# A quarter of an FFT stage moved into the first FFN group, and casts and PSUM emptyings handed to other engines

## The chip, the cores and the metric

One core of a Trainium2 chip. The metric is the device time of one execution in microseconds (us). Each run lists the mean granted TensorE clock, and executions with a mean of 1.000 are some 1.3 us shorter than those with 0.998. "Full-clock runs" below are those with 1.000; where a tenth of a per cent matters I compare these alone.

## The reference, cut to what matters

```python
X = np.fft.rfft(x, axis=1)                       # x: 8 batches x 3008 x 256
Y = X * (filt_r + 1j * filt_i)[None]
y = np.fft.irfft(Y, n=3008, axis=1).astype(np.float32)
h = np.maximum(y.reshape(24064, 256) @ w_in, 0)  # w_in: 256 x 2048
return (h * h @ w_out).astype(np.float32)        # w_out: 2048 x 256
```

## The kernel before

The FFT is done by matmuls in stages: A (x to u, through memory), B (u to the spectrum, times the filter: "products"), P (products to ze, through memory as dZ), Y (zt to yt). The FFN is done in groups of 512 tokens with 8 slots each: first layer (psH), relu on ScalarE, squaring on VectorE, second layer (psO, TensorE). TensorE leaves its results in PSUM tiles, which ScalarE or VectorE then "empties", that is, copies into a tile in SBUF. The code calls a piece of 512 fp32 columns of such a tile a "bank". The FFN of one batch hides the FFT of the next. Only the start is exposed: batch 0's FFT, three quarters of stage A of batch 1, and FFN group 0, whose first layer has no second layer beside it. The parts that the change and the argument touch:

```python
p_u = ctx.enter_context(tc.tile_pool(name="p_u", bufs=3))   # u tiles, and the two sSPx tables
def psF(name): ...   # [128, 512] fp32, 2 buffers;  psO: likewise 2;  psH: [128, 2, 512], 2 buffers

def place_f(im, k, *engs, rotate=False):       # builds 4 columns of the filter, Fr or Fi
    ...
        t = psH(f"psf_{im}_{k}")
        banks, groups = [t[:, 0, :], t[:, 1, :]], [(t, 0)]
    ...                                        # matmuls into the two banks
    for t, i in groups:                        # each group emptied by engs[i % len(engs)]
        ...

def unit_a(b, a):                              # one sixteenth of stage A
    c, i = divmod(a, 4)
    if i == 0:
        us[(b, c)] = p_u.tile([96, 8, D], F16, tag="u", name=f"u_{b}_{c}")
    ps = psF(f"psA_{b}_{a}")
    ...                                        # two matmuls
    if a % 2 == 0: nc.scalar.copy(out=o, in_=pv)
    else:          nc.vector.tensor_copy(out=o, in_=pv)
    if i == 3: write_u(b, c)

# in the plan of batch 1, by slot (0 to 7 are group 0):
            for k in range(4):
                put((4, 5, 7, 7)[k], 1, cast_wout, k, nc.vector)
        t0 = 2 if b == 1 else 6
        for a in range(12 if b == 1 else 0, 16):
            put(t0 + a // 2, a % 2, unit_a, b, a)          # units 12 to 15: slots 8 and 9

# the start:
    for k in range(7):
        ...                                                # unit_b, place_f(1, ..), unit_p0
        if k < 4:
            place_f(0, k + 2, nc.scalar)                   # an Fr bank
    cast_wide(1, 2, nc.vector, nc.scalar)
    read_z(0, 0); load_wout(0); read_z(0, 1); load_wout(1) # zt, and 2 MB of W_out
    for c in (0, 2, 1): chunk_a(1, c)                      # stage A of batch 1, chunks 0, 2, 1
    for c in (0, 2, 1): write_u(1, c)
    for n in range(4): unit_y(0, n)
```

Of the kernel before, what the change touches and what calls it, by code (L numbers as in the profile page):

```python
# [110 lines left out]
def kernel(  # L111
# [9 lines left out]
    nc = tc.nc  # L121
    B, S, D = x.shape
# [34 lines left out]
    def psF(name):  # L157
        return pps.tile([128, 512], F32, tag="psF", name=name, bufs=2)

    def psO(name):  # L160
        return pps.tile([128, 2, 256], F32, tag="psO", name=name, bufs=2)

    def psH(name):
        return pps.tile([128, 2, 512], F32, tag="psH", name=name, bufs=2)
# [4 lines left out]
    def bank_pair(name):  # L169

        k = npair[0] % 4
        npair[0] += 1
        if k < 2:
            t = psH(name)
            return [t[:, 0, :], t[:, 1, :]], [(t, 0)]
        ts = [psF(f"{name}_{i}") if k == 2 else psO(f"{name}_{i}").rearrange("p a d -> p (a d)")
              for i in range(2)]
        return ts, [(t.unsqueeze(1), i) for i, t in enumerate(ts)]
# [42 lines left out]
    def cast(eng, out, in_):  # L221
        (eng.copy if eng is nc.scalar else eng.tensor_copy)(out=out, in_=in_)

    def cast_wide(b, k, *engs):
        t = p_x16.tile([128, 8, D], F16, tag="x16", name=f"xw16_{b}_{k}")
        for i in range(2):
            m = slice(4 * i, 4 * i + 4)
            cast(engs[i], t[:, m, :], xw32[(b, k)][:, m, :])
        xw16[(b, k)] = t
# [36 lines left out]
    ps = psO("warm").rearrange("p a d -> p (a d)")  # L266
# [2 lines left out]

    f16s = []  # L270

    def place_f(im, k, *engs, rotate=False):

        if rotate:
            banks, groups = bank_pair(f"psf_{im}_{k}")
        else:
            t = psH(f"psf_{im}_{k}")
            banks, groups = [t[:, 0, :], t[:, 1, :]], [(t, 0)]
        for i in range(4):
            c = 4 * k + i  # L280
            e0, e1 = D * c, D * (47 - c)
            cuts = [0] + [d for d in range(1, D)
                          if (e0 + d) % QF == 0 or (c and (e1 + d) % QF == 0)] + [D]
            for d0, d1 in zip(cuts, cuts[1:]):
                o = banks[i // 2][:, (i % 2) * D + d0:(i % 2) * D + d1]
                q, a = divmod(e0 + d0, QF)
                nc.tensor.matmul(o, sPF[:, PQ.index((0, q)), :], f16s[0][:, im, a:a + d1 - d0],  # L287
                                 start=True, stop=False)
                q, a = divmod(e1 + d0, QF) if c else (0, QF + d0)
                nc.tensor.matmul(o, sPF[:, PQ.index((1, q)), :], f16s[0][:, im, a:a + d1 - d0],  # L290
                                 start=False, stop=True)
        for t, i in groups:
            n = t.shape[1]
            eng = engs[i % len(engs)]
            dst = sF[:, im, 4 * k + 2 * i:4 * k + 2 * i + 2 * n, :]
            src = t.rearrange("p t (a d) -> p (t a) d", d=D)
            if eng is nc.scalar:
                eng.activation(out=dst, in_=src, func=AF.Copy, scale=sign[:, 0:1] if im else 1.0)  # L298
            elif im:
                eng.tensor_scalar_mul(out=dst, in0=src, scalar1=sign[:, 0:1])  # L300
            else:
                eng.tensor_copy(out=dst, in_=src)
# [15 lines left out]
    def cast_win():  # L318
        for t, k, c in wins:
            nc.gpsimd.tensor_copy(out=sWin[:, k, c], in_=t)  # L320
# [22 lines left out]
    def write_u(b, c):  # L343
        nc.sync.dma_start(
            out=dU[b].rearrange("(m q) d -> q m d", q=96)[:, 8 * c:8 * c + 8, :],
            in_=us.pop((b, c)))

    def unit_a(b, a):
# [5 lines that stand above are left out]
        m = slice(2 * i, 2 * i + 2)  # L354
        if b == 1:
            nc.tensor.matmul(ps[0:96, :], s1[:, c // 2, :], xw16[(b, 2 * (c % 2))][:, m, :],
                             start=True, stop=False)
            nc.tensor.matmul(ps[0:96, :], s1[0:120, 2 + c, :], xw16[(b, 1)][0:120, m, :],
                             start=False, stop=True)
        else:  # L360
            nc.tensor.matmul(ps[0:96, :], sSA, x16s[(b, c)][:, m, :], start=True, stop=True)  # L361
        o = us[(b, c)][:, 2 * i:2 * i + 2, :]
        pv = ps[0:96, :].rearrange("p (a d) -> p a d", d=D)
        if a % 2 == 0:
            nc.scalar.copy(out=o, in_=pv)  # L365
        else:
            nc.vector.tensor_copy(out=o, in_=pv)  # L367
        if i == 3:
            write_u(b, c)
# [102 lines left out]
    def unit_p0(k):  # L472

        if k == 0:
            zes[0] = p_h2.tile([128, NC, D], F16, tag="h2", name="ze_0")
        ze = zes[0][:, 4 * k:4 * k + 4, :]
        ps = psH(f"psP_0_{k}")
        for i in range(4):
            c2 = 4 * k + i
            prod = prods[(0, c2 // 2)]  # L480
            for v, w in enumerate((sSP[:, c2, :], sSPx[c2 // 12][:, c2 % 12, :])):
                nc.tensor.matmul(ps[:, i // 2, (i % 2) * D:(i % 2) * D + D], w,
                                 prod[:, v, i % 2, :], start=(v == 0), stop=(v == 1))
        nc.scalar.copy(out=ze, in_=ps.rearrange("p t (a d) -> p (t a) d", d=D))
        nc.sync.dma_start(
            out=dZ[0].rearrange("(s p) d -> p s d", p=128)[:, 4 * k:4 * k + 4, :],
            in_=ze)
# [22 lines left out]
    def read_z(b, c, ks=(0, 1)):  # L510
        zt = ztiles[c]
        v = dZ[b].rearrange("(q j) d -> q j d", j=NM)
        for k in ks:
            nc.sync.dma_start(out=zt[64 * k:64 * k + 48],
                              in_=v[48 * k:48 * k + 48, 8 * c:8 * c + 8, :])
        zts[(b, c)] = zt
# [93 lines left out]
    def fft_plan(b):  # L610

        plan = {}

        def put(r, place, f, *a):
            plan.setdefault((r, place), []).append((f, a))

        if b == 1:
            for n in range(4, 16):
                put(n if n < 8 else n + 2 if n < 12 else 2 * n - 7, n % 2, unit_y, 0, n)
            for k in range(4):  # L620
                put((4, 5, 7, 7)[k], 1, cast_wout, k, nc.vector)
        t0 = 2 if b == 1 else 6
        for a in range(12 if b == 1 else 0, 16):
            put(t0 + a // 2, a % 2, unit_a, b, a)
        put(10 if b == 1 else 14, 1, read_u, b)
        t0 = 14 if b == 1 else 19
        for p in range(12):
            r = t0 + (17 if b == 1 else 18) * p // 11
            put(r, 0, unit_b, b, p)
            put(r, 0, unit_s, b, p)  # L630
            put(r + 2, 1, unit_p, b, p)
        t0 = 34 if b == 1 else 40
        for c in range(4):
            put(t0, 1, read_z, b, c)
        if b + 1 < B:
            for c in range(2):
                put(t0 - 13, 1, load_x, b + 1, c)
            for c in range(4):
                r = t0 - 8 + 3 * c
                put(r, 1, cast_x, b + 1, c)  # L640
                if c < 2:
                    put(r, 1, load_x, b + 1, c + 2)
        for n in range(16):
            put((38 if b == 1 else 45) + n // 2, n % 2, unit_y, b, n)
        return plan
# [32 lines left out]
    turn_u(2, nc.scalar)  # L678
    turn_u(3, nc.vector)
    place_f(0, 0, nc.scalar, rotate=True)  # L680
    for eng, e in ((nc.vector, slice(0, 1024)), (nc.gpsimd, slice(1024, 2048)),
                   (nc.scalar, slice(2048, QF))):
        cast(eng, f16s[0][:, 1, e], f32s[1][:, e])
    turn_u(4, nc.vector)
    place_f(0, 1, nc.scalar, rotate=True)
    turn_u(5, nc.vector)
    place_f(1, 0, nc.scalar, nc.vector, rotate=True)
# [4 lines left out]
        nc.gpsimd.tensor_copy(out=sSPx[-1][0:64, o, :], in_=sSP[64:128, c, :])  # L692
        nc.gpsimd.tensor_copy(out=sSPx[-1][64:128, o, :], in_=sSP[0:64, c, :])
    cast_win()
    for k in range(2):
        cast_wide(1, k, nc.gpsimd, nc.gpsimd)
    for k in range(7):
        if k < 6:
            unit_b(0, 2 * k)
            if k < 5:  # L700
                place_f(1, k + 1, nc.scalar)
            unit_b(0, 2 * k + 1)
        if k > 0:
            unit_p0(k - 1)
        if k < 4:
            place_f(0, k + 2, nc.scalar)
    cast_wide(1, 2, nc.vector, nc.scalar)
    read_z(0, 0)
    load_wout(0)
    read_z(0, 1)  # L710
# [17 lines left out]
    for s in range((NG + 1) * SLOTS):  # L728
        g, k = divmod(s, SLOTS)
# [40 lines left out]
```

## Time and profile before

The median at the prediction was 794.04 us (793.07 to 794.68, 3 runs).

| event in the trace of before | us |
|---|---|
| twelfth product of batch 0 ends | 40.40 |
| last store of ze (dZ) landed | 44.49 |
| first psY matmul; first psH matmul | 48.26; 49.71 |
| last W_out landed; chunk 0 of u written | 56.35; 57.59 |
| second psH matmul of group 1 (the row "x3") | 59.76 |
| first product of batch 1 | 73.74 |
| span | 791.9 |

A landing is the sixteenth increment of a transfer's semaphore.

One more view, ScalarE's timeline in batch 0's loop (columns: start, duration, engine, line, operation, output and input, shape, count; a bracket holds the idle time before it and what ended it):

```profile
28.83 1.02 ACT L298 ACTIVATE sF<-psf 128x1024 f16<-128x1024 f32 x1
29.93 1.11 ACT L298 ACTIVATE sF<-psf,sign 128x1024 f16<-128x1024 f32 x1
31.02 1.01 ACT L484 CAST ze<-psP 128x1024 f16<-128x1024 f32 x1
```

A whole Fr bank pair, a Fi bank pair and a ze, without a gap: 3.14 us of each cycle of 3.33. That is what the change wants to shorten.

### The profile page before, as it was taken

To read this page: it belongs to the slowest core of one execution; us is meant where nothing else is said; L and a number is where in the kernel's file an instruction comes from. 1 tells how busy PE (TensorE), PEld (TensorE's weight loads), DVE (VectorE), ACT (ScalarE), POOL (GpSimd) and SP (SyncE) were. 2 spreads that over 40 slices of the span, in tenths; PEclk is the share of its full clock that TensorE was granted. 3 is DMA by queue.
4 is the path that set the end of the run, shared out by engine and by line. 5 is a ranking of instruction groups with operands and counts; after the bars stand their busy time and mean duration, and the time that the engine had idled before them with its cause. 6 is when DMAs were issued, how large, how long until landed. Compare 5 with 4: busy or idle time off the path is not lost.

```text
span 791.9 us, 14822 instructions
## 1 busy us (share of the span) xinstructions
PE 778.9 (98%) x6102; PEld 552.5 (70%) x6102; DVE 550.3 (69%) x897; ACT 557.4 (70%) x711; POOL 23.6 (3%) x36
## 2 busy tenths in 40 slices
PE   8989999999999999999999999999999999999998
PEld 5746667667676777867777676776767677676666
DVE  6866994579755897559965699556995579553342
ACT  3976776777777777767776777676777777776664
POOL 3800000000000000000000000000000000000000
PEclk9999999999999999999999999999999999999999
DMA  9994554346814557154562555424563332611111
GB/s 363 368 260 153 146 157 111 93 135 167 205 42 112 167 155 180 48 173 135 132 167 65 163 147 155 112 80 148 159 180 86 97 133 66 147 40 41 41 41 54
DMA packets 88571, 107.32 MB, mean 136 GB/s; under 512 B 6336, under 2 KB 79040, under 8 KB 84288
## 3 DMA queue, kind: packets, MB, share of 16 engines
q1 hardware_dynamic: 88296, 106.19, 46.5%
q8 instruction: 48, 0.79, 0.4%
q10 hardware_dynamic: 144, 0.18, 0.1%
q14 instruction: 19, 0.16, 0.1%
q0 software_dynamic: 64, 0.00, 0.0%
HBM read 58.12 MB, written 48.23 MB: 134 GB/s over the span
## 4 chain that ended last, share of the span: by engine, by line
PE 89%; DVE 6%; DMA 3%; ACT 1%; SPq 0%; issue 0%; DVEq 0%; ACTq 0%
PE psO L579 40%; PE psH L562 38%; PE psA L361 3%; PE psY L532 2%; PE psB L445 2%; DMA f<-in_filt_i_dram 2%; PE psP L496 2%; DVE prod L453 2%; DVE h L570 1%; DMA wout<-in_moe_w_out_dram 1%; PE psf L287 1%; PE psf L290 1%; DVE yf L467 0%; ACT sF L298 0%; DVE yf L461 0%; ACT h L566 0%
## 5 line engine op out<-in xcount | busy, mean ns | idle before, releaser
L566 ACT ACTIVATE h<-psH 128x1024 f16<-128x1024 f32 x376 | 384.9, 1024 | 189.3 <-PE psH L562 186.7
L579 PE MATMUL psO<-sWout,h 128*128 128x256 f16 x3008 | 388.9, 272 | 0.6 <-DVE h L570 0.6
L562 PE MATMUL psH<-yt,sWin 128*128 128x512 f16 (+7 forms) x1728 | 386.9, 351 | 1.6 <-DVE yt L541 0.7
L579 PEld LDWEIGHTS <-h 128*128 128x128 f16 x3008 | 290.6, 98 | 79.1 <-DVE h L570 0.9
L570 DVE TENSOR_TENSOR h<-h 128x1024 f16<-128x1024 f16 x376 | 252.6, 685 | 104.7 <-ACT h L566 104.5
L562 PEld LDWEIGHTS <-sWin 128*128 128x128 f16 x1728 | 159.5, 98 | 101.7 <-issue 3.3
L453 DVE TENSOR_TENSOR prod<-psB,sF 128x1024 f16<-128x1024 f32 x84 | 102.3, 1218 | 2.8 <-PE psB L445 2.8
L541 DVE CAST yt<-psY 128x376 f16<-128x376 f32 x62 | 34.0, 549 | 59.4 <-PE psY L532 59.4
L367 DVE CAST u<-psA 96x512 f16<-96x512 f32 x50 | 34.3, 687 | 47.3 <-PE psA L361 45.1
L498 ACT CAST ze<-psP 128x512 f16<-128x512 f32 x84 | 49.1, 585 | 17.2 <-PE psP L496 14.7
L590 ACT COPY ost<-psO 128x512 f32<-128x512 f32 (+1 forms) x96 | 55.8, 581 | 6.8 <-PE psO L579 5.3
L532 PE MATMUL psY<-sC,zt 112*128 112x94 f16 x512 | 42.4, 205 | 1.4 <-DMA zt<-dZ 1.4
L532 PEld LDWEIGHTS <-zt 112*128 112x128 f16 x512 | 35.1, 98 | 11.6 <-issue 1.6
L467 DVE TENSOR_TENSOR yf<-prod,yf 128x512 f16<-128x512 f16 x84 | 35.7, 425 | 2.9
L361 PE MATMUL psA<-x,sC 94*96 94x512 f16 x96 | 36.6, 382 | 0.0
L445 PE MATMUL psB<-ut,sSB 128*128 128x256 f16 x192 | 36.5, 273 | 0.0
L496 PE MATMUL psP<-yf,sSP 128*128 128x256 f16 x168 | 32.1, 272 | 0.5 <-DVE prod L453 0.3
L539 ACT CAST yt<-psY 128x376 f16<-128x376 f32 x66 | 30.9, 468 | 2.0 <-issue 1.7
L445 PEld LDWEIGHTS <-sSB 128*128 128x128 f16 x192 | 18.5, 98 | 19.5
L340 DVE CAST x<-x 94x2048 f16<-94x2048 f32 x24 | 29.2, 1216 | 0.0
L365 ACT CAST u<-psA 96x512 f16<-96x512 f32 x50 | 28.6, 572 | 0.0
L460 DVE COPY yf<-prod 64x512 f16<-64x512 f16 x84 | 24.3, 289 | 2.9
(65 smaller groups left out, 253.2 us busy)
## 6 DMA issues: line engine op xcount, KB each, us to landing
x<-in_x_dram SPq DMA_DIRECT2D x20, 768.0 KB
zt<-dZ SPq DMA_DIRECT2D x64, 192.0 KB
dU<-u SPq DMA_DIRECT2D x28, 384.0 KB
dZ<-ze SPq DMA_DIRECT2D x28, 384.0 KB
out_dram<-ost SPq DMA_DIRECT2D x66, 128.0 KB
out_dram<-ost SPq DMA_DIRECT2D x31, 256.0 KB
ut<-dU SPq DMA_DIRECT2D x7, 1024.0 KB
xw<-in_x_dram SPq DMA_DIRECT2D x6, 1024.0 KB
```

Of the source, the lines that this page charges most:

```text
L361: nc.tensor.matmul(ps[0:96, :], sSA, x16s[(b, c)][:, m, :], start=True, stop=True)
L445: nc.tensor.matmul(ps[:, i * D:(i + 1) * D], sSB[:, 2 * p + i, :], uts[b][:, 2 * p + i, :], start=True, stop=True)
L453: nc.vector.tensor_mul(out=prod, in0=ps.rearrange("p (a d) -> p a d", d=D).unsqueeze(1).to_broadcast([128, 2, 2, D]), in1=sF[:, :, 2 * p:2 ...
L467: nc.vector.tensor_add(out=yf, in0=prod[:, 0], in1=yf)
L496: nc.tensor.matmul(ps[:, i * D:(i + 1) * D], sSP[:, 2 * p + i, :], yf[:, i, :], start=True, stop=True)
L498: nc.scalar.copy(out=zes[(b, c)][:, 2 * i6:2 * i6 + 2, :], in_=ps.rearrange("p (a d) -> p a d", d=D))
L532: nc.tensor.matmul(ps[:, 94 * jj:94 * jj + 94], zt[:, 4 * (g % 2) + jj, dt * 128:(dt + 1) * 128], sSY, start=True, stop=True)
L562: nc.tensor.matmul(ps[:, i, o:o + n], sWin[:, dt, jt * 128:(jt + 1) * 128], yts[b][:, dt, r:r + n], start=(dt == 0), stop=(dt == 1))
L566: nc.scalar.activation(out=h2[:, 2 * s:2 * s + 2, :], in_=ps, func=AF.Relu)
L570: nc.vector.tensor_mul(out=v, in0=v, in1=v)
L579: nc.tensor.matmul(pso[g][:, t % 2, :], h2s[g][:, jt, t * 128:(t + 1) * 128], sWout[:, jt, :], start=(jt == 0), stop=(jt == NJT - 1))
L590: nc.scalar.copy(out=ost[:, h0:h0 + step, :], in_=pso[g][:, h0:h0 + step, :])
```

## The change

Its intent: (1) share the Fr banks, and the last ze, between ScalarE and VectorE, and put the last x casts on idle GpSimd, so that batch 0's spectrum ends sooner; (2) take the W_out casts from VectorE to GpSimd; (3) run units 12 to 15 of stage A in slots 1 to 4 of group 0, where TensorE has holes, instead of in slots 8 and 9, where it is full. All four of these units are then emptied by VectorE (before, ScalarE took two of them), and four psY units come two slots earlier.

```diff
-    def place_f(im, k, *engs, rotate=False):
+    def place_f(im, k, *engs, rotate=False, halves=False):
...
-            banks, groups = [t[:, 0, :], t[:, 1, :]], [(t, 0)]
+            banks = [t[:, 0, :], t[:, 1, :]]
+            groups = [(t[:, i:i + 1, :], i) for i in range(2)] if halves else [(t, 0)]
...                                              (unit_a)
-        if a % 2 == 0:
+        if a % 2 == 0 and b > 1:
             nc.scalar.copy(out=o, in_=pv)
...                                              (unit_p0: the last ze)
-        ps = psH(f"psP_0_{k}")
+        if k == 5:
+            ps = [psF("psP_0_5a"), psF("psP_0_5b")]
...                                              (for k < 5 as before: one psH tile, emptied by ScalarE)
-        nc.scalar.copy(out=ze, in_=ps.rearrange("p t (a d) -> p (t a) d", d=D))
+        else:
+            nc.scalar.copy(out=ze[:, 0:2, :], in_=ps[0].rearrange("p (a d) -> p a d", d=D))
+            nc.scalar.copy(out=ze[:, 2, :], in_=ps[1][:, 0:D])
+            nc.vector.tensor_copy(out=ze[:, 3, :], in_=ps[1][:, D:2 * D])
...                                              (the plan of batch 1)
-                put(n if n < 8 else n + 2 if n < 12 else 2 * n - 7, n % 2, unit_y, 0, n)
+                put(n if n < 12 else 2 * n - 7, n % 2, unit_y, 0, n)
-                put((4, 5, 7, 7)[k], 1, cast_wout, k, nc.vector)
-        t0 = 2 if b == 1 else 6
+                put((1, 2, 4, 5)[k], 1, cast_wout, k, nc.gpsimd)
+        t0 = 6
-            put(t0 + a // 2, a % 2, unit_a, b, a)
+            put(a - 11 if b == 1 else t0 + a // 2, a % 2, unit_a, b, a)
...                                              (the start)
-    for k in range(2):
+    for k in range(3):
         cast_wide(1, k, nc.gpsimd, nc.gpsimd)
-            place_f(0, k + 2, nc.scalar)
-    cast_wide(1, 2, nc.vector, nc.scalar)
+            place_f(0, k + 2, nc.scalar, nc.vector, halves=True)
```

More of the change, by code (lines that the diff above doesn't have):

```diff
@@ L476, in unit_p0 @@
         ze = zes[0][:, 4 * k:4 * k + 4, :]
-        ps = psH(f"psP_0_{k}")
+        if k == 5:
+            ps = [psF("psP_0_5a"), psF("psP_0_5b")]
+        else:
+            t = psH(f"psP_0_{k}")
+            ps = [t[:, 0, :], t[:, 1, :]]
         for i in range(4):
@@ L481, in unit_p0 @@
             for v, w in enumerate((sSP[:, c2, :], sSPx[c2 // 12][:, c2 % 12, :])):
-                nc.tensor.matmul(ps[:, i // 2, (i % 2) * D:(i % 2) * D + D], w,
+                nc.tensor.matmul(ps[i // 2][:, (i % 2) * D:(i % 2) * D + D], w,
                                  prod[:, v, i % 2, :], start=(v == 0), stop=(v == 1))
-        nc.scalar.copy(out=ze, in_=ps.rearrange("p t (a d) -> p (t a) d", d=D))
+        if k < 5:
+            nc.scalar.copy(out=ze, in_=t.rearrange("p t (a d) -> p (t a) d", d=D))
+        else:
+            nc.scalar.copy(out=ze[:, 0:2, :], in_=ps[0].rearrange("p (a d) -> p a d", d=D))
+            nc.scalar.copy(out=ze[:, 2, :], in_=ps[1][:, 0:D])
+            nc.vector.tensor_copy(out=ze[:, 3, :], in_=ps[1][:, D:2 * D])
         nc.sync.dma_start(
```

## The prediction

> **What bounds the kernel now.** I read the page first (busy shares and chain), then a table of engine busy time by stretch, then each engine's timeline from 22 to 75 us, because every line of the diff acts there. The page:
>
> ```profile
> PE 778.9 (98%) x6102; PEld 552.5 (70%) x6102; DVE 550.3 (69%) x897; ACT 557.4 (70%) x711; POOL 23.6 (3%) x36
> ...
> PE 89%; DVE 6%; DMA 3%; ACT 1%; SPq 0%; issue 0%; DVEq 0%; ACTq 0%
> ```
>
> TensorE sets the time: 89% of the chain that ended last. So a change in the first 75 us is worth what it does to the moment at which a given piece of the main TensorE stream is reached. The stretches:
>
> ```profile
> 22.00:32.00 10.00, 9.65 (x93) 8.27 (x94) 9.37 (x10) 9.02 (x10) 8.50 (x14) 1.00 1.04 412
> 32.00:42.00 10.00, 9.01 (x80) 7.24 (x78) 7.63 (x8) 8.22 (x10) 7.13 (x10) 1.00 0.78 278
> 42.00:49.70 7.70, 5.72 (x44) 3.48 (x43) 4.45 (x6) 5.01 (x9) 0.00 (x0) 1.00 0.74 202
> 49.70:59.80 10.10, 8.91 (x50) 4.07 (x50) 7.12 (x13) 8.40 (x10) 0.00 (x0) 1.00 1.11 315
> 59.80:73.20 13.40, 13.40 (x99) 8.90 (x99) 7.42 (x13) 8.28 (x11) 0.00 (x0) 1.00 0.46 138
> ```
>
> Columns: stretch, length, busy us of TensorE, its weight loads, VectorE, ScalarE, GpSimd, then clock, DMA share, GB/s. Three regimes. (a) 22 to 42, batch 0's spectrum (Fr/Fi banks, products, ze): TensorE, VectorE and ScalarE all 76 to 97% busy. (b) 42 to 49.7: TensorE waits for ze to go out to memory and come back as zt. (c) 49.7 to 59.8 is FFN group 0, with first matmuls alone, so TensorE has holes; from 59.8 it has none. The change moves TensorE work from the full stretch into the one with holes. The DMA share in (c), 1.11, is the highest: the queue is full just there.
>
> **What the Trainium skill says.** "VectorE: DVE Perf Modes", section "Why PSUM operands drop a tier": a PSUM operand in fp32 gets no speed-up. The trace agrees: a 96x512 VectorE emptying takes 0.69 us and a 128x1024 product 1.22, against 0.57 and 1.02 for ScalarE's emptying of these widths. "GPSIMD Engine Reference", section "4.1 Engine selection": one-input work is roughly line-rate there. The trace: four 128x1024 casts in 3.99 us, 1.0 each, against 0.68 on VectorE. "PSUM — Partial Sum Buffer", section "Engine vs sequencer instructions": the queues of ScalarE, VectorE and GpSimd are strict FIFO. I use that below; every timeline here agrees. "TensorE: Matmul & The Clock Gate", section "What's actually happening": after an idle window of about 3.4 us the clock can halve. Here the clock column is 1.00, and the longest TensorE wait in stretches (a) to (c) is 1.42 us, so this trace tests nothing of it; the changed kernel may.
>
> **Part 1, Fr banks and last ze on two engines, x casts to GpSimd (22 to 44 us).** VectorE before:
>
> ```profile
> 24.42 7.06 DVE L453 TENSOR_TENSOR prods<-psB,sF 128x1024 f16<-128x1024 f32 x6
> 32.44 2.35 DVE L453 TENSOR_TENSOR prods<-psB,sF 128x1024 f16<-128x1024 f32 x2 [0.96 <-ACT ze L484]
> 35.77 4.62 DVE L453 TENSOR_TENSOR prods<-psB,sF 128x1024 f16<-128x1024 f32 x4 [0.98 <-ACT ze L484]
> 40.30 0.68 DVE L222 CAST xw<-xw 128x1024 f16<-128x1024 f32 x1
> ```
>
> Twelve products (14.03 us) and 1.94 us of waits end at 40.40; then the last ze matmuls (0.6 us), one ScalarE emptying from 41.07 to 42.09, and the last store. Now VectorE also empties half of four Fr banks: 4 x 0.62 (0.69 alone, some 0.62 back to back, as in a pair of 1.28) = 2.5 us. The two waits hold only 1.9, so VectorE becomes the loop's bound: 24.42 + 14.03 + 2.5 = 40.95, about 0.1 more for small waits, 41.05: 0.65 later. ScalarE loses 4 x 0.45 (1.02 to 0.57), but the TensorE cycle of 3.33 us there runs through the emptying of the Fi bank (1.11), which stays whole. At the end the last ze is 256 columns on each engine, about 0.42 by extrapolation from 1.22 and 0.69, in place of 1.02: 0.60 earlier. Sum: +0.65 - 0.60, about nil. The x casts leave VectorE (0.68) and ScalarE (1.05), but lie in the wait for zt; on GpSimd they run from 39.14 to about 41.2, before their reader at about 45. Worth 0.
>
> **Part 2, W_out cast to GpSimd.** Four x 0.61 us leave VectorE in (c), where it was 70% busy. The last landing of W_out is at 56.35 (the sixteenth increment of its semaphore), so GpSimd ends near 58.4, before the first use. Worth nearly 0 by itself: the last yt emptying of group 0 waits for the squaring before it anyway.
>
> **Part 3, the quarter of stage A into group 0.** Gain: four units x 2 matmuls x 0.217 us = 1.74 us of TensorE leave the full stretch. Shifting four psY units within it changes no sum.
>
> The price is a buffer. The u tiles have 3 buffers and rotate: two hold the sSPx tables, then u of chunks 0, 2, 1, then chunk 3, the moved quarter. Chunk 3 therefore takes chunk 0's buffer and its first emptying must wait until chunk 0 has been written to memory. The compiled kernel before has just that wait on that instruction. It costs nothing there, since that emptying comes at 61.91. When does chunk 0 land?
>
> ```profile
> 45.05 0.39 SPq L328 DMA_DIRECT2D wout<-in_moe_w_out_dram  x1
> 45.49 1.03 SPq L514 DMA_DIRECT2D zt<-dZ  x2
> 46.57 0.43 SPq L328 DMA_DIRECT2D wout<-in_moe_w_out_dram  x1
> 47.10 7.71 SPq L344 DMA_DIRECT2D dU<-u  x3
> ```
>
> It is issued at 47.10, but behind 2 MB of W_out on one queue: its 512-byte packets start only at about 55.3, after the last of W_out, and the sixteenth increment of its semaphore comes at **57.59**. The change leaves that order alone. The moved unit 12 would be ready to be emptied at about 52, so VectorE stands from there to 57.59. Behind it, in order, stand squarings and yt emptyings. Unit 14 needs unit 12's PSUM bank (psF, two of them), so TensorE stops at it, from about 54.2. Compare TensorE before:
>
> ```profile
> 54.17 1.02 PE L562 MATMUL psH<-yt,sWin 128*128 128x512 f16 x4 [0.20 <-ACT h L566]
> ...
> 57.60 1.02 PE L562 MATMUL psH<-yt,sWin 128*128 128x512 f16 x4
> 58.46 0.33 PE L532 MATMUL psY<-sC,zt 112*128 112x94 f16 x4
> 58.88 0.38 PE L562 MATMUL psH<-yt,sWin 128*128 128x512 f16 x1
> 59.76 0.81 PE L562 MATMUL psH<-yt,sWin 128*128 128x512 f16 x3 [0.50 <-DVE yt L541]
> ```
>
> Played forward with the durations above (slot 4 is 54.17, slot 7 is 57.60, slot 8 begins group 1 and needs unit y7's emptying): VectorE empties unit 12 until 58.3, then squaring, unit 13, squaring, unit 14, squaring, until 61.3. TensorE: unit 14 at 58.33, slot 4 at 58.8, y4 at 59.6, then unit 15 waits for unit 14's bank, 60.7; slot 5 at 61.2, slot 6 at 62.2, slot 7 at 63.3 (after relu 5), y7 at 64.2. VectorE: unit 15 until 62.0, squaring 4, y5 until 63.1, squarings 5 and 6 (after relu 6, 64.3) until 65.0, y7 until 65.5. Group 1's second matmul then starts at 65.5, not 59.76: **+5.7 us**. From there TensorE is full in both kernels, minus 1.74 until the first product of batch 1 (slot 14): 5.7 - 1.74 = +4.0. After it the 73 to 112 us stretch is bound by TensorE and VectorE together (38.31 and 37.47 of 38.80 us), and the rest by TensorE: nothing gives the delay back.
>
> Total: 794.0 + 4.0 + 0.0 = **798.0 us**.
>
> **Rivals.** (1) The move works as meant: no wait, since the buffer is free or lands sooner. Group 0 stretches by about 1 us (slots of 0.87 + 0.43 on TensorE in place of 1.08 set by ScalarE), 1.74 leave: about 793. For it: TensorE's holes in (c), 10.1 - 8.9 of 10.1 us and more below the pipelined count. Against it: the landing at 57.59. I give it 12%. (2) The Fr split pays, because ScalarE was the loop's bound in (a): up to 4 x 0.3 us plus the 0.6 of the last ze. For it: ScalarE 9.02 of 10 us. Against: VectorE at 9.37 gets the work. With the stall: 796 to 797. (3) The hole of some 4 us halves TensorE's clock for a few us: 799 to 801, about one in five. (4) VectorE's added halves delay the loop by more than 1 us, through psP banks that now wait for VectorE: 799.
>
> **Range and chances.** Mass around 798: rivals 1 and 2 stretch below, 3 and 4 above: 794.5 to 800.5. Two per cent is 15.9 us; nothing here is near it either way: faster 0.5%, slower 1%.
>
> **What would show it.** Right: VectorE idle from about 52.5 to 57.6 before an emptying of psA into u, ended by a dU write; a TensorE hole of some 4 us before the third psA unit; the first group-1 matmuls complete near 65; products in 24 to 41 us with gaps filled and the last store issued within 0.4 us of 42.1; no psA after group 0. Wrong: the emptyings in group 0 start by 54; or the last store leaves before 41.5; or the clock column below 1.00 after 50 us; or the delay shrinks between 73 and 112 us.

## The result, and the profile after

The changed kernel took 801.37 us (median; 800.47 to 802.26, 5 runs), the kernel before 793.47 (793.07 to 794.68, 5 runs). The ratio is 1.0097, with a 95% interval of 1.0083 to 1.0111. A ratio here is the mean time of one kernel's runs over that of the other's in the same rounds, so it is not quite the ratio of the two medians. The change costs 7.9 us by the medians; the prediction said 4.0, with 800.5 as the top of its range. The profiled execution is the fastest of the five, 800.47, and its span is 798.6: 6.7 us over before.

The page after, busy shares and chain:

```profile
PE 780.3 (98%) x6102; PEld 552.8 (69%) x6102; DVE 552.5 (69%) x899; ACT 554.2 (69%) x709; POOL 30.1 (4%) x42
...
PE 90%; DMA 5%; DVE 3%; ACT 1%; issue 0%; ACTq 0%; DVEq 0%; SPq 0%
```

Nothing of the whole changes: TensorE still bounds the kernel. DMA's share of the chain rose from 3 to 5%. The table by stretch (length, busy us of TensorE, weight loads, VectorE, ScalarE, GpSimd, then clock, DMA share, GB/s):

```profile
42.50:51.20 8.70, 7.26 (x52) 4.50 (x52) 4.45 (x6) 4.52 (x9) 0.00 (x0) 1.00 0.71 200
51.20:60.40 9.20, 4.64 (x20) 2.07 (x20) 2.79 (x5) 3.98 (x4) 4.30 (x4) 0.99 1.09 306
60.40:63.60 3.20, 3.18 (x11) 1.43 (x11) 3.15 (x5) 0.42 (x1) 0.21 (x1) 0.50 0.91 257
63.60:68.20 4.60, 3.97 (x27) 1.98 (x26) 3.59 (x6) 4.22 (x6) 0.00 (x0) 1.00 0.36 92
```

Group 0 took 10.1 us before, with TensorE at 8.9. Now it begins at 51.2 and ends at 68.2, 17 us, and in its first 9.2 us TensorE works 4.6 and VectorE 2.8. The third row shows a clock of 0.50. VectorE's timeline:

```profile
53.86 1.36 DVE L580 TENSOR_TENSOR h<-h 128x1024 f16<-128x1024 f16 x1 [1.95 <-ACT h L576]
59.68 0.69 DVE L368 CAST u<-psA 96x512 f16<-96x512 f32 x1 [4.46 <-DMA dU<-u]
```

This is the predicted stall: 4.46 us before the first emptying of psA into u, ended by the write of dU from the same buffer (it landed at 59.56). Unpredicted is the row above it: a squaring takes 1.36 us, where it took 0.69. TensorE's timeline:

```profile
55.20 1.03 PE L572 MATMUL psH<-yt,sWin 128*128 128x512 f16 x4
60.42 0.59 PE L357 MATMUL psA<-xw,sC 128*96 128x512 f16 x1 [4.19 <-DVE u L368]
...
61.23 1.91 PE L572 MATMUL psH<-yt,sWin 128*128 128x512 f16 x4
...
68.22 0.81 PE L572 MATMUL psH<-yt,sWin 128*128 128x512 f16 x3 [0.45 <-DVE yt L551]
```

The hole of 4.19 us stands before the third psA unit, as predicted. After it, four matmuls take 1.91 us instead of 1.03. Cutting the trace at the edges of the slow stretch shows why (same table, other stretches):

```profile
56.79:60.20 3.41, 0.00 (x0) 0.00 (x0) 0.52 (x1) 0.50 (x1) 1.62 (x2) 1.00 1.14 343
60.20:63.61 3.41, 3.19 (x11) 1.43 (x11) 3.35 (x6) 0.43 (x1) 0.41 (x1) 0.50 0.93 264
```

A window of 3.41 us without one matmul is followed by a window of 3.41 us at half clock. This is what the prediction had from the page on TensorE's clock gate as a possibility, with a window of about 3.4 us; the trace agrees, with 3.41 us for both windows. One such window lowers the mean clock of a run by 0.5 x 3.41 / 795 = 0.002; all five runs have a mean of 0.994 to 0.997.

The start lost time as well, which the prediction did not have. In batch 0's loop, the two halves of an Fr bank pair (ScalarE's view, then VectorE's):

```profile
33.22 0.60 ACT L299 ACTIVATE sF<-psf 128x512 f16<-128x512 f32 x1
```

```profile
30.39 0.69 DVE L303 CAST sF<-psf 128x512 f16<-128x512 f32 x1 [0.78 <-ACT sF L299]
...
33.85 0.69 DVE L303 CAST sF<-psf 128x512 f16<-128x512 f32 x1 [0.51 <-ACT sF L299]
...
37.21 0.69 DVE L303 CAST sF<-psf 128x512 f16<-128x512 f32 x1 [0.41 <-ACT sF L299]
```

VectorE does not work beside ScalarE; it begins when ScalarE has ended, after 0.51 us of idleness. Three such waits, 1.70 us together, stand in the loop. The compiled program has a wait for ScalarE's count on VectorE's instruction: both halves are views of one PSUM tile. The last ze does the same (43.11 to 43.48 on ScalarE, then 43.52 on VectorE). So the twelfth product ends at 42.43, not 40.40.

The events of the two traces side by side:

| event | before | after | later by |
|---|---|---|---|
| twelfth product ends | 40.40 | 42.43 | 2.03 |
| last dZ landed | 44.49 | 46.35 | 1.86 |
| first psH matmul | 49.71 | 51.24 | 1.53 |
| group 1, second psH matmul | 59.76 | 68.22 | 8.46 |
| first product of batch 1 | 73.74 | 80.39 | 6.65 |
| span | 791.9 | 798.6 | 6.7 |

Read from below: after 73 us nothing is lost or given back. The 1.8 us between the last rows but one is TensorE work that left the full stretch (predicted 1.74). Group 0 costs 8.46 - 1.53 = 6.93 (predicted 5.7), the start 1.5 to 1.9 (predicted 0).

### The profile page after: what moved, and what is told of

It is laid out like the page before. It is cut to its first block, busy times and chain, and to the rows that moved or that the text cites. A ratio compares the mean times of both kernels' runs of the same rounds, so it can differ in the third digit from the quotient of the medians.

```text
span 798.6 us, 14818 instructions
## 1 busy us (share of the span) xinstructions
PE 780.3 (98%) x6102; PEld 552.8 (69%) x6102; DVE 552.5 (69%) x899; ACT 554.2 (69%) x709; POOL 30.1 (4%) x42
## 4 chain that ended last, share of the span: by engine, by line
PE 90%; DMA 5%; DVE 3%; ACT 1%; issue 0%; ACTq 0%; DVEq 0%; SPq 0%
PE psO L589 40%; PE psH L572 39%; PE psA L362 3%; PE psY L542 3%; PE psB L446 2%; PE psP L506 2%; DMA sSP<-cSP 2%; DMA dU<-u 1%; DVE prod L454 1%; DVE h L580 1%; DMA xw<-in_x_dram 1%; DMA win<-in_moe_w_in_dram 1%; PE psP L487 1%; ACT h L576 0%; ACT ze L490 0%; DVE yf L468 0%
## 5 line engine op out<-in xcount | busy, mean ns | idle before, releaser
L576 ACT ACTIVATE h<-psH 128x1024 f16<-128x1024 f32 x376 | 385.0, 1024 | 195.2 <-PE psH L572 192.5
```

Of the source, the lines that this page charges most:

```text
L576: nc.scalar.activation(out=h2[:, 2 * s:2 * s + 2, :], in_=ps, func=AF.Relu)
```

## The experiments

The theory: the start loses its 2 us because two engines that empty one PSUM tile take turns, and group 0 loses the rest through the u buffer, its hole and the half clock. Rivals: the loop is simply bound by VectorE's added work; the loss in group 0 comes from the order of the transfers, or from GpSimd slowing VectorE. Twelve kernels ran, on different chips; every one gave the right output. The kernel before ran nine times beside each lot: 793.67, 793.62 and 793.27 us (medians), and in its full-clock runs 793.60, 793.54 and 793.27.

| kernel | median (range), us | ratio | full-clock runs, less before's |
|---|---|---|---|
| fr_only | 796.85 (795.94 to 797.01) | 1.0031 | +2.4 |
| quarter_only | 798.77 (798.57 to 799.79) | 1.0062 | none at 1.000 |
| after_ubuf | 796.17 (795.20 to 796.69) | 1.0024 | +1.7 |
| after_warm | 800.60 (800.39 to 800.91) | 1.0081 | +7.2 |
| fr_apart | 793.66 (793.18 to 793.82) | 0.9995 | +0.1 |
| ze_apart | 793.57 (793.46 to 794.83) | 0.9999 | 0.0 |
| quarter_ubuf | 794.49 (793.58 to 794.79) | 1.0004 | +0.4 |
| quarter_order | 794.81 (794.46 to 795.85) | 1.0013 | +1.2 |
| wout_pool | 794.03 (793.86 to 796.02) | 1.0014 | +0.7 |
| quarter_ubuf_dve | 792.69 (792.51 to 794.31) | 0.9994 | -0.6 |
| best_dve | 794.48 (793.17 to 796.57) | 1.0015 | +1.0 |
| best_warm | 794.27 (793.89 to 796.12) | 1.0014 | +0.7 |

The last column is the median of the full-clock runs less that of the kernel before in the same lot (two to four such runs each, so its last tenths are rough). With the runs at 0.999 counted too, quarter_ubuf becomes +0.7; no other figure moves by more than 0.2.

### fr_only: part 1 alone

The changed kernel with the plan of batch 1 as before:

```diff
-                put((1, 2, 4, 5)[k], 1, cast_wout, k, nc.gpsimd)
+                put((4, 5, 7, 7)[k], 1, cast_wout, k, nc.vector)
-            put(a - 11 if b == 1 else t0 + a // 2, a % 2, unit_a, b, a)
+            put(t0 + a // 2, a % 2, unit_a, b, a)          # t0 = 2 for b == 1; unit_a and unit_y as before
```

> Part 1 alone: Fr halves, last ze on two engines, x casts on GpSimd; the plan of the main loop as before. Theory A: VectorE's half of a PSUM tile waits for ScalarE's half of the same tile, so the two engines take turns and the loop of 24 to 42 us is no faster and its end later; the changed kernel's first FFN matmul came 1.5 us later than before's (51.24 against 49.71), so this run should be 1.5 to 1.9 us slower than before, 795.0 to 795.5, at clock 1.000. Rival (the prediction as made): the halves run side by side and this part is worth about nil, 793 to 794. If it is slower by 4 us or more, the hole in group 0 is not the main cause.

Measured: 796.85, and the last dZ landed at 46.35, exactly as in the whole change. Part 1, which the prediction had at nil, costs 2.4 us at full clock. Three of the five runs had a clock of 0.998, the profiled one among them. Its stretches:

```profile
48.33:51.74 3.41, 1.82 (x25) 1.29 (x25) 1.34 (x3) 1.63 (x4) 0.00 (x0) 1.00 0.99 290
51.74:55.16 3.42, 3.28 (x8) 1.13 (x8) 0.78 (x2) 1.12 (x2) 0.00 (x0) 0.50 1.07 239
```

Here the window ahead of the half clock was not empty: TensorE was busy 1.82 of 3.41 us. This is the wait for zt with the small psY matmuls after it, which every kernel here has. So half clock followed the hole of over 4 us in every run of the changed kernel (by the mean clocks), and it follows this half-busy stretch in some executions. TensorE's busy time does not decide it alone: in quarter_order a window with less work, 1.65 of 3.41 us (60.61 to 64.02), was not followed by half clock.

### quarter_only: parts 2 and 3 alone

The kernel before with the changed plan and unit_a (the diff of the plan, above).

> Parts 2 and 3 alone: the last quarter of stage A in group 0 and the W_out cast on GpSimd; the prologue as before. Theory A: the u buffer of chunk 0 is not free before its write lands (57.6 us), TensorE stands 4 us and then gets half a clock for 3.4 us: 5 to 6.5 us slower than before, 798.5 to 800, clock 0.994 to 0.997. The sum of this and the part 1 run should be the whole change (+7.9) within 0.7 us. Rival: parts interact, the prologue's delay being hidden or doubled, and the sum is off by over 1 us.

Measured: 798.77, clocks of 0.995 to 0.998. The hole is there without part 1:

```profile
58.55 0.58 PE L356 MATMUL psA<-xw,sC 128*96 128x512 f16 x1 [4.51 <-DVE u L367]
```

Half clock ran from 58.15 to 61.56, group 1's second matmul came at 66.26, 6.5 us later than before, and the span is 796.7, 4.8 over before. By medians the two parts cost 3.2 and 5.1 us, 8.3 together, against 7.9 for the whole: they add, within the spread.

### after_ubuf: the whole change with a free buffer for the moved quarter

```diff
-            us[(b, c)] = p_u.tile([96, 8, D], F16, tag="u", name=f"u_{b}_{c}")
+            pool, tag = (p_x32, "x32") if b == 1 else (p_u, "u")
+            us[(b, c)] = pool.tile([96, 8, D], F16, tag=tag, name=f"u_{b}_{c}")
```

> The changed kernel, with u of chunk 3 in a buffer of another pool that has long been free. Theory A (buffer wait): no idle VectorE before the first psA emptying of group 0, no TensorE hole of over 1 us, clock 1.000, and the time falls by 6 to 7.5 us to 794 to 795.5 (part 1's +1.7, a group 0 longer by about 1 us, minus 1.74). Rival B: GpSimd's W_out casts[...] (one squaring took 1.36 in place of 0.69 us), are what holds group 0 up: then it stays above 798.

Measured: 796.17, 5.2 us below the changed kernel, though chunk 0 of u still landed at 59.64.

```profile
58.19 0.38 PE L358 MATMUL psA<-xw,sC 128*96 128x512 f16 x1 [0.48 <-DVE u L369]
```

The hole of 4.19 is a wait of 0.48 and the clock is 1.00. The buffer, not the move, made the stall. The rival of the expectation (the W_out casts hold group 0 up: above 798) falls. What remains at full clock, +1.7, is no more than part 1's cost.

### after_warm: the whole change with matmuls of zeros in the hole

```diff
+        if b == 1 and a == 14:
+            wps = psO("keep").rearrange("p a d -> p (a d)")
+            for _ in range(18):
+                nc.tensor.matmul(wps, zero, sF[:, 0, 0:2, :], start=True, stop=True)
```

> The changed kernel with 18 matmuls on zeros (0.215 us each, 3.9 us) ahead of the third psA unit, which fill the hole and compute nothing that is used. Theory A with the clock: the buffer wait stays, but the clock stays at 1.000 and the time falls by 0.7 to 2.5 us, to 799 to 800.7, with less spread between runs. Rival: the half clock runs while TensorE waits for VectorE anyway and costs nothing: 801 to 802.

Measured: 800.60, with clocks of 0.998 to 1.000.

```profile
56.44 4.05 PE L357 MATMUL keep<-sF,zero 128*128 128x512 f16 x18
61.30 0.38 PE L361 MATMUL psA<-xw,sC 128*96 128x512 f16 x1 [0.81 <-DVE u L372]
...
68.67 0.81 PE L576 MATMUL psH<-yt,sWin 128*128 128x512 f16 x3 [0.45 <-DVE yt L555]
```

The zeros fill the hole, 0.81 us of it is left, and the unit after it runs at full speed (0.38, not 0.59). This takes away the half clock behind the hole and keeps the stall. The gain is 0.8 us by the medians. The traces give less: chunk 0 landed at 60.44 here and at 59.56 in the changed kernel, and from there to the second psH matmul of group 1 (68.67 and 68.22) it is 8.23 us here and 8.66 there, 0.4 apart. The changed kernel's fastest run, 800.47, even lies inside this kernel's range. So the half clock behind the hole costs some 0.4 to 0.8 us, less than the 1.7 us that a window at half speed could cost: VectorE has a backlog of emptyings and squarings at that time, for which TensorE waits again here (0.87 us at the fourth unit).

### fr_apart: part 1 with a PSUM tile for each engine

Shown against part 1 of the changed kernel:

```diff
+            if halves:
+                banks = [psF(f"psf_{im}_{k}_a"), psO(f"psf_{im}_{k}_b").rearrange("p a d -> p (a d)")]
+                groups = [(t.unsqueeze(1), i) for i, t in enumerate(banks)]
...
-            ps = [psF("psP_0_5a"), psF("psP_0_5b")]
+            ps = [psF("psP_0_5a"), psF("psP_0_5b"), psO("psP_0_5c").rearrange("p a d -> p (a d)")]
...                                              (the fourth column of the last ze goes to psP_0_5c, for VectorE)
```

> Part 1 alone again, but each half of an Fr bank, and each of the last ze's three pieces, has a PSUM tile of its own, so that no engine waits for the other's read. Theory A (turn-taking at a shared PSUM tile is what made part 1 slow): ScalarE's and VectorE's halves overlap in time, the last ze store lands at 44.0 to 44.9 us in place of 46.35, and the time is within 1 us of before at equal clock, 793 to 794.5. Rival (VectorE's added work, 2.5 us, is the cost, or the psum slots): store at 45.5 or later, 795 or more.

Measured: 793.66, ratio 0.9995 (0.9982 to 1.0009), against fr_only's 796.85. Both engines in one view:

```profile
33.10 0.69 DVE L306 CAST sF<-psf_b 128x512 f16<-128x512 f32 x1
...
33.13 0.60 ACT L302 ACTIVATE sF<-psf_a 128x512 f16<-128x512 f32 x1
```

Now the halves run at once. The cycle is 3.06 us (VectorE's halves start at 26.97, 30.04, 33.10, 36.16), against 3.4 in the changed kernel and 3.33 before. The same work and the same engines, with no turns to take: VectorE's half now waits for TensorE's count alone, and VectorE's added work by itself is not the cost. This kernel also takes the Fr banks out of the psH tiles, and what that is worth was not tested apart; but the loop is 1.28 us shorter than the changed kernel's, and the waits for ScalarE that are gone were 1.70. The prediction's own sums fit this kernel. Its loop of twelve products runs from 24.62 to 41.38, 16.76 us, where the prediction had 24.42 to 41.05, 16.63. From there to the landing of the last dZ, at 44.92, are 3.54 us against 4.09 before: a gain of 0.55, predicted 0.60. In the changed kernel the loop is 18.04 us and this gain is 0.17.

### ze_apart: only the last ze in three tiles, and the x casts on GpSimd

```diff
-            place_f(0, k + 2, nc.scalar, nc.vector, halves=True)
+            place_f(0, k + 2, nc.scalar)            # and the last ze in three tiles, as in fr_apart
```

> Only the end of part 1: the last ze in three tiles of their own on two engines, and the x casts on GpSimd; Fr banks as before. Theory A: the last store leaves 0.5 to 0.7 us sooner (landing 43.8 to 44.0 in place of 44.49), and the time falls by 0.1 to 0.7 us, less what the first yt emptying loses (0.4 us in the changed kernel): 793.0 to 793.7. Rival: the zt read does not follow, and nothing moves.

Measured: 793.57, ratio 0.9999. The last dZ landed at 43.94, 0.55 earlier than before, and none of it reached the time. VectorE's first emptying of psY into yt started at 48.67, some 0.4 us after its matmuls, and the second psH matmul waited 0.35 us for it. The same lateness is in the changed kernel and in fr_only (50.90 and 50.82), not in fr_apart (49.02, right after its matmuls). Why is open: in these kernels yt takes a buffer that GpSimd's x cast read last, so more waits stand before it, but fr_apart has that too.

### quarter_ubuf: parts 2 and 3 with the free buffer

The changed plan on the kernel before, with the buffer of after_ubuf.

> Parts 2 and 3 alone with u of chunk 3 in the free buffer. Theory A: no hole; group 0 about 1 us longer, 1.74 us gone from the full stretch: 0.5 to 1.0 us faster than before at equal clock, 792.6 to 793.2. Rival: GpSimd's W_out casts slow the squarings and eat it: 793.5 or more.

Measured: 794.49, +0.4 at full clock (+0.7 with the traced run, which is the slowest of the five and at 0.999). The move without its stall should have gained about 1 us (the prediction's first rival). It did not. VectorE, GpSimd and TensorE:

```profile
57.76 1.53 DVE L571 TENSOR_TENSOR h<-h 128x1024 f16<-128x1024 f16 x1
```

```profile
57.17 3.49 POOL L333 CAST sWout<-wout 128x1024 f16<-128x1024 f32 x2 [1.84 <-DMA wout<-in_moe_w_out_dram]
```

```profile
62.31 0.81 PE L563 MATMUL psH<-yt,sWin 128*128 128x512 f16 x3 [1.45 <-DVE yt L542]
```

While GpSimd casts W_out, a squaring takes 1.53 us instead of 0.69, and a cast 1.75 instead of 1.0: each slows the other. The last yt emptying stands behind the squarings, and TensorE waits 1.45 us for it. The Trainium skill names a reason, on the page "SBUF — State Buffer", section "Who interferes with whom": "only the shared port pair causes contention, and it's an exclusive lock", with GpSimd on VectorE's second pair. The trace fits: a squaring reads two operands of SBUF, while an emptying of psA (one operand, in PSUM) in the middle of a cast still took 0.68. That the two take turns, and do not share, can be read too: in the seven traces with W_out casts on GpSimd, each of the 20 squarings that began while such a cast ran ended 0.54 us after the cast's end, whether it took 0.81 or 1.53 in all, and all 12 emptyings of PSUM that lay inside a cast kept their length of 0.53 to 0.69.

### quarter_order: chunk 0 of u computed and written before W_out is read

```diff
     read_z(0, 0)
+    chunk_a(1, 0)
+    write_u(1, 0)
     load_wout(0)
     read_z(0, 1)
     load_wout(1)
-    for c in (0, 2, 1):
+    for c in (2, 1):
         chunk_a(1, c)
```

> Parts 2 and 3 alone, three u buffers as in the change, but chunk 0 of u is computed and its write issued before W_out is read. Theory A (the landing behind W_out is the cause): chunk 0 lands by 51 us in place of 57.6, no hole of over 1 us; W_out and the second zt come about 1.1 us later; 792.6 to 794. Rival: the wait is another one, the hole stays and the time is 797 or more.

Measured: 794.81, +1.2 at full clock. With the three buffers as they are, the earlier write removes the 4 us hole too. But zt and W_out then land later, and TensorE waits 0.70 and 0.97 us for zt and 1.06 for yt. So the order of the queue is the other half of the stall's cause, and mending it there costs more than taking another buffer.

### wout_pool: part 2 alone

```diff
-                put((4, 5, 7, 7)[k], 1, cast_wout, k, nc.vector)
+                put((1, 2, 4, 5)[k], 1, cast_wout, k, nc.gpsimd)
```

> The kernel before with one part alone: the four W_out casts on GpSimd in slots 1, 2, 4 and 5 of group 0, the quarter still spread over the group as before. Theory (GpSimd's casts slow VectorE's squarings): the first two squarings of group 0, 0.69 us in the kernel before, take 1.2 to 1.6 us each while a GpSimd cast runs; VectorE gives up four casts but gets later to psY and psA, and the time is within 0 to +2 us of before at like clock. Rival (as the prediction had it, the place of the casts is worth nearly nothing in itself): squarings stay at 0.7 us, and the time is within 0.3 us of before.

Measured: 794.03, +0.7 at full clock. VectorE, then GpSimd:

```profile
52.51 4.05 DVE L570 TENSOR_TENSOR h<-h 128x1024 f16<-128x1024 f16 x4 [0.22 <-ACT h L566]
```

```profile
51.66 2.96 POOL L333 CAST sWout<-wout 128x1024 f16<-128x1024 f32 x2 [12.47 <-DMA wout<-in_moe_w_out_dram]
```

Four squarings take 4.05 us; one by one they are 1.22, 1.44, 0.68 and 0.69. The first of all, at 51.59, began before a cast and took 0.69. My expectation had the first two slowed, so the place was wrong by one and the size (1.2 to 1.6) was right. The rival (nearly nothing, within 0.3 us) falls: VectorE gave up four casts of 0.61 and the kernel got slower.

### quarter_ubuf_dve: the move with the free buffer, W_out casts left on VectorE

```diff
-                put((1, 2, 4, 5)[k], 1, cast_wout, k, nc.gpsimd)      # quarter_ubuf
+                put((4, 5, 7, 7)[k], 1, cast_wout, k, nc.vector)      # as in the kernel before
```

> The quarter early with a free u buffer, and the four W_out casts left on VectorE in slots 4, 5, 7, 7 as before. Theory (it is the GpSimd casts that ate the gain of the move): squarings back at 0.7 us, no wait of TensorE over 0.6 us for psA, first second-layer matmul of group 1 (the x3 row) at 58.5 to 61.5 us, the time 0.5 to 1.5 us below the same kernel with the casts on GpSimd (794.49), so 792.5 to 794. Rival (the move itself is worth nothing, because VectorE, with four emptyings of u and four casts, is late for group 0's last squaring): that matmul at 62 or later and 794 to 795.5.

Measured: 792.69. The four full-clock runs took 792.51 to 792.70 and the eight of the kernel before beside them 793.10 to 793.45: 0.6 us faster, with no overlap. Over all runs the ratio is 0.9994 (0.9982 to 1.0007), because each kernel has a run at 0.998. VectorE and TensorE:

```profile
56.98 0.68 DVE L571 TENSOR_TENSOR h<-h 128x1024 f16<-128x1024 f16 x1
```

```profile
60.44 0.81 PE L563 MATMUL psH<-yt,sWin 128*128 128x512 f16 x3 [0.71 <-DVE yt L542]
```

Squarings are back at 0.68, the wait for yt falls from 1.45 to 0.71, and the first product of batch 1 comes at 72.7 (73.7 before, 74.7 in quarter_ubuf). Compared through their own kernels before, the GpSimd casts cost 0.4 + 0.6 = 1.0 us here, or 1.3 with the runs at 0.999.

### best_dve and best_warm: the parts put together

best_dve is fr_apart with the plan of quarter_ubuf_dve. best_warm adds five matmuls of zeros before the first unit_y:

```diff
+    keep = psO("keep").rearrange("p a d -> p (a d)")
+    for _ in range(5):
+        nc.tensor.matmul(keep, zero, sF[:, 0, 0:2, :], start=True, stop=True)
     for n in range(4):
         unit_y(0, n)
```

> The parts that paid or cost nothing put together: Fr halves and pieces of the last ze in PSUM tiles of their own, x casts on GpSimd, the quarter early with a free u buffer, W_out casts on VectorE. Theory (gains add): about the free-buffer quarter with casts on VectorE, 792.5 to 794, dZ's last landing near 44.9. Rival (no gain left, all within the spread of before): 793.3 to 794.5.

> As the run before it, with five matmuls of zeros (0.22 us each, into a psO bank nobody reads) ahead of the wait for the first zt. Theory A (some executions lose 1 to 1.5 us to a half clock that begins in this wait): all five runs at a mean clock of 0.999 or 1.000 and the spread of the five under 0.6 us. Rival (the slower executions come from elsewhere, or the matmuls only delay the first psY): spread and clocks as without them, or 0.3 us more.

Measured: 794.48 and 794.27. The gains do not add; best_dve is 1.0 us slower than before at full clock, beyond the theory's range and at the edge of the rival's.

```profile
62.87 0.33 PE L547 MATMUL psY<-sC,zt 112*128 112x94 f16 x4 [1.22 <-DMA zt<-dZ]
```

TensorE waits 1.22 us for the third quarter of zt, whose second half lands at 62.74; in quarter_ubuf_dve it lands at 61.02 and nobody waits. The last of W_out, ahead of it on the queue, is late by as much (57.34 against 56.13), although the last dZ landed only 0.3 later (44.76 against 44.45). fr_apart shows the same lateness (57.98 and 63.63), and uses that zt later. Why W_out takes longer there is open. In best_warm the zeros shrank no spread (793.89 to 796.12, clocks of 0.997 to 1.000), so its theory A is not confirmed: one of the five runs (796.12, clock 0.997) still has a slow stretch, as one of best_dve has, so five matmuls in that wait do not keep the clock up in every execution.

## Why the prediction was right or wrong

**Right: the direction, and the stall of part 3.** The buffer that chunk 3 shares with chunk 0, the landing behind 2 MB of W_out, VectorE's wait (4.46 us), the hole before the third psA unit (4.19) and the 1.74 us of TensorE work that leave the full stretch (1.8 in the traces) are all as played forward, and nothing was given back later. Rival 1 ("the buffer is free or lands sooner": about 1 us faster) does not come out with the free buffer alone (quarter_ubuf, +0.4); it needs the casts back on VectorE as well, and then gives 0.6 (quarter_ubuf_dve). The predicted stall was a little too short: in quarter_only, which has no part 1, group 1's second psH matmul comes 6.5 us later, predicted 5.7. Of these 0.8, the traces put 0.3 to 0.4 on the half clock, 0.2 on a squaring slowed by a cast (0.87 at 58.42) and 0.1 on the landing (57.69).

**Wrong: "Sum: +0.65 - 0.60, about nil."** Part 1 cost 1.86 us by the landing of the last dZ and 2.4 in full-clock runs (two of them; no trace shows where the rest lies). The step took for granted that two engines empty two halves of a PSUM tile at once. They take turns. So the loop of products took 18.04 us instead of the 16.63 worked out, and the last ze gained 0.17 instead of 0.60. With separate tiles (fr_apart) both terms come out within 0.15 us of the prediction, and the sum is indeed about nil: the last dZ lands 0.43 later than before, and the time is +0.1. Rival 4 (delay over 1 us) had the size, and by another way than the psP banks that it named. It also moved the stall, as the landing of chunk 0 went from 57.59 to 59.56.

**Wrong in its chance: rival 3, the half clock, "about one in five".** It came in all five runs of the changed kernel and in all of quarter_only, by their mean clocks. The prediction's own hole of some 4 us was longer than the window it quotes, which spoke for more. The length alone does not explain ten of ten: a hole of 4.19 us holds a whole window of 3.41 us at only (4.19 - 3.41) / 3.41, some 23%, of the places where a window can begin (an estimate that takes every place as equally likely), so windows that are only partly empty must count too, as in fr_only. It was mis-sized as a chance; as a cost, it is the 0.4 to 0.8 us of after_warm.

**Wrong in size: part 2, "Worth nearly 0 by itself".** The step counted what leaves VectorE and not what GpSimd takes from it: +0.7 us alone, about 1.0 beside the moved quarter. Inside the stall of the changed kernel it is the slowed squaring, some 0.2 us by the trace; no run has the stall without the casts on GpSimd.

The sum by traces: 4.8 (parts 2 and 3) + 1.9 (part 1) = 6.7, the difference of the spans. The medians differ by 1.2 more. The other four runs of the changed kernel have mean clocks of 0.994 to 0.997, and 0.002 is one more window at half speed; no trace shows where it fell in them, so this last piece is argued and not shown; and one of the four, 801.16, has the traced run's 0.997, so in it 0.7 us must come from elsewhere.

**One reading that does not show what it is quoted for.** The prediction sets VectorE's times beside ScalarE's for the missing speed-up with PSUM operands. Its own lines have the fit comparison: VectorE's cast of 1024 fp32 columns out of SBUF took 0.68 us (40.30), and its emptying of half as many out of PSUM 0.69.

## What to carry to other kernels

Before an emptying is split between two engines, give each engine a PSUM tile of its own, and look in the compiled program or the timeline for one engine's count in the other's wait. Before work is moved earlier, ask which buffer it will take and when that buffer's last reader, often a transfer at the end of a queue, is done. An idle engine is not a free one: measure what its work does to the neighbour's instructions, and count a TensorE hole of over 4 us as a hole plus a stretch at half speed, as it was in all ten runs here that had it unfilled; in a shorter or half-filled one the stretch may come or not.

## What the Trainium skill lacked or had wrong

- "TensorE: Matmul & The Clock Gate", section "What's actually happening": it speaks of an idle window. It does not say how idle. A window with TensorE busy 0.00 of 3.41 us was followed by half clock, and so was one with 1.82 of 3.41 (fr_only), in some executions and, by the mean clock, not in others of the same kernel. One with 1.65 (quarter_order) was not.
- "GPSIMD Engine Reference", section "4.1 Engine selection": one-input work is called roughly line-rate. The casts took 1.0 us each alone, 1.75 beside VectorE's squarings, and slowed a squaring from 0.69 to as much as 1.53. The table does not say so beside its advice; the contention stands in other sections of that page and on the SBUF page.
- Two engines that take turns at one PSUM tile: "PSUM — Partial Sum Buffer", section "PSUM bank collisions raise a hardware error ⚠️", says that a compiler's scheduler adds a dependency between ScalarE and VectorE where both touch one bank, as both do in the last ze. It does not have the case of the Fr pair, two halves in two banks of one tile, where the compiled program had the wait all the same: the second half began 0.03 us after the first ended in the changed kernel, and at the same time (33.10 and 33.13) with two tiles, worth 2.4 us of the whole.
